# Sliding-window decode attention on one core: K and V in 32 KB rows, word transposes on VectorE, PV on four row groups

## The chip, the core and the metric

The kernel runs on one core of a Trainium2 chip. The core has a matrix engine (TensorE, "PE" in the profile, with its weight loads shown as "PEld"), VectorE ("DVE"), ScalarE ("ACT"), GpSimd ("POOL") and SyncE ("SP"), which here only issues transfers. 16 DMA engines carry data between HBM and the core's SBUF. Matmuls write PSUM, eight banks of 2 KB in each of 128 partitions; VectorE and ScalarE copy results out of it. The metric is the device time of one execution in microseconds; lower is better.

## What is computed

32 sequences each decode one token. The window is the last 512 keys of a cache of 2048. Four query heads share one key/value head (32 query heads, 8 KV heads, head size 128).

```python
W = min(4096, max(256, Sk // 4))                       # 512
q = (x @ wq).reshape(B, 1, 32, 128).transpose(0, 2, 1, 3)
k = jnp.repeat(k_cache[:, :, Sk - W:, :], 4, axis=1)
v = jnp.repeat(v_cache[:, :, Sk - W:, :], 4, axis=1)
p = softmax(einsum("bhqd,bhkd->bhqk", q, k) * 128 ** -0.5)
o = einsum("bhqk,bhkd->bhqd", p, v)
return o.transpose(0, 2, 1, 3).reshape(B, 1, 4096) @ wo
```

All arrays are bf16. The windows of K and of V are 33.5 MB each, wq and wo 4.2 MB each: 75.5 MB are read once.

## The kernel before

**Loads.** SP issues everything but x. The four pieces of wq (1 MB, rows of 8 KB) come first. Then `load_k(b)` (L136) and `load_v(b - 5)` (L144) alternate over the 32 batches, each in two halves of four KV heads, 512 KB in 128 rows of 4 KB: a partition holds 16 successive keys of one head (head c, key group s, with partition = 4 s + c). There are six K buffers and eight V buffers; a load waits until PE has finished with the batch that held its buffer. wo follows in eight pieces of 512 KB (L155), into the space of wq.

**Queries.** PE turns x, multiplies by wq with the weight columns as the stationary operand (L221), so that q comes out with the head dimension on the partitions; VectorE and ACT copy it to `QT_sb` (L353, L427). POOL lays each batch's q into `QBD` (L203), a zeroed block layout, so that eight matmuls give the scores of all heads of a batch.

**Scores.** For each batch, `transposes(b)` (L243) turns K in 32 PE transposes with a permutation as the moving operand, into four PSUM banks; VectorE copies three of these (L361) and ACT one (L435) into `KT_sb`. `scores(b)` (L260) multiplies 128 x 32 slices of `QBD` with 512 columns of `KT_sb`, four heads on four column groups of the array, and collects four batches in one bank `S_ps` of 128 rows (32 heads x 4 batches) by 512 keys.

**Softmax, for four batches ("a quad").** VectorE takes the row maximum (L367) and scales it (L369); ACT computes exp with the row sums (L443); VectorE takes the reciprocal (L375) and writes the normalised probabilities, spread out over four column slots, into `P_ex` (L383: four instructions of 32 partitions). PE transposes `P_ex` (L275), ACT copies it to `PT_sb` (L453).

**PV and output.** For each batch, 32 matmuls (L293) with V as the stationary operand (128 x 128) and 16 columns of `PT_sb`. VectorE copies the result, 32 columns, to `oT_sb` (L397). At the end band matmuls (L305) reorder `oT_sb` for the output projection (L337), 128 matmuls against wo; VectorE and ACT copy the result (L418, L473) and SP stores it (L161).

The engines run their own instruction lists in order; semaphores tie them together. On PE the order is transposes(it), scores(it - 1), pv_matmuls(it - 6), and every fourth iteration the transposes of P.

Of the kernel before, what the change touches and what calls it, by code (L numbers as in the profile page):

```python
# [12 lines left out]
def bass_standalone__sliding_block_cached__sampling_kernel(  # L13
# [15 lines left out]
    G = HKV  # L29
    G4 = 4  # L30
    NR = 16
    NS = 32
    DKT = D // 128
    SCALE = float(DH) ** -0.5
    P = 128

    NK = 6
    NV = 8
    NKT = 3
    NQB = 8  # L40
    LEAD = 5
    PVLAG = 6
    NQUAD = B // 4
    NHG = HQ // 4
    SELCUT = 28

    with ExitStack() as es:  # L47
        sb = lambda name, shape, dt: es.enter_context(nc.sbuf_tensor(name, shape, dt))
        ps = lambda name, shape, dt: es.enter_context(nc.psum_tensor(name, shape, dt))
        sem = lambda name: es.enter_context(nc.semaphore(name))  # L50

        w_sb = sb("w_sb", [P, DKT * HD], BF16)
        wq_sb = w_sb[:, :].rearrange("p (kt n) -> p kt n", kt=DKT)
        wo_sb = w_sb[:, :].rearrange("p (g i n) -> p g i n", g=NHG, i=4)
        K_sb = sb("K_sb", [P, NK, 2, NR, DH], BF16)
        V_sb = sb("V_sb", [P, NV, 2, NR, DH], BF16)
        KT_sb = sb("KT_sb", [P, NKT, 2, NR, G4, NS], BF16)
        QT_sb = sb("QT_sb", [P, HQ, B], BF16)
        QBD = sb("QBD", [P, NQB, G, 32], BF16)
        P_f32 = sb("P_f32", [P, W], F32)  # L60
        P_ex = sb("P_ex", [P, NR, NS, G4], BF16)
        PT_sb = sb("PT_sb", [P, 2, NR, P], BF16)
        oT_sb = sb("oT_sb", [P, HQ, B], BF16)
        o_sel = sb("o_sel", [P, 4, NHG, B], BF16)
        band = sb("band", [P, 4, 224], BF16)
        xT_sb = sb("xT_sb", [P, DKT, 32], BF16)
        ident = sb("ident", [P, P], BF16)
        perm = sb("perm", [P, G4, NS], BF16)
        x_sb = sb("x_sb", [32, D], BF16)
        out_sb = sb("out_sb", [32, 4, 128], BF16)  # L70
        maxv = sb("maxv", [P, NQUAD], F32)
        negmax = sb("negmax", [P, NQUAD], F32)
        sums = sb("sums", [P, NQUAD], F32)
        recip = sb("recip", [P, NQUAD], F32)
        junk = sb("junk", [P, 2], F32)

        KT_ps = ps("KT_ps", [P, 4, 1024], BF16)
        S_ps = ps("S_ps", [P, 512], F32)
        PT_ps = ps("PT_ps", [P, 2, 1024], BF16)
        QO_ps = ps("QO_ps", [P, 512], F32)  # L80
# [3 lines left out]
        sem_wo = [sem(f"sem_wo{i}") for i in range(NHG)]  # L84
        sem_k = [[sem(f"sem_k{i}_{h}") for h in range(2)] for i in range(NK)]
        sem_v = [sem(f"sem_v{i}") for i in range(NV)]
        sem_out = sem("sem_out")
        pe_xT = sem("pe_xT")
        pe_qt = sem("pe_qt")
        pe_T = [sem(f"pe_T{t}") for t in range(4)]  # L90
        pe_S = sem("pe_S")
        pe_PT = sem("pe_PT")
        pe_PV = sem("pe_PV")
        pe_fin = sem("pe_fin")
        pe_sel = sem("pe_sel")
        dve_sel = sem("dve_sel")
        act_sel = sem("act_sel")
        act_out = sem("act_out")
        pool_band = sem("pool_band")
        pool_perm = sem("pool_perm")  # L100
        pool_ex = sem("pool_ex")
        dve_xT = sem("dve_xT")
        dve_qt = sem("dve_qt")
        act_qt = sem("act_qt")
        dve_T = sem("dve_T")
        act_T = sem("act_T")
        dve_sm = sem("dve_sm")
        dve_sm2 = sem("dve_sm2")
        dve_P = sem("dve_P")
        dve_oT = sem("dve_oT")  # L110
        act_exp = sem("act_exp")
        act_PT = sem("act_PT")
        dve_out = sem("dve_out")
        act_warm = sem("act_warm")
        pool_init = sem("pool_init")
        pool_qbd = sem("pool_qbd")
        nc.scalar.dma_start(x_sb[:, :], x.rearrange("b s d -> b (s d)")).then_inc(sem_x, 16)
# [3 lines left out]
        def score_row(h, j):  # L121
            return 16 * h + 4 * j

        def cache_rows(cache, b, h):
            return cache[b, 4 * h:4 * h + 4, SK - W:, :].rearrange("g (s r) d -> s g (r d)", s=NS)

        @block.sync
        def _(sp):
# [3 lines left out]
            def load_k(b):  # L132
                if b >= NK:
                    sp.wait_ge(pe_T[3], b - NK + 1)
                for h in range(2):
                    sp.dma_start(  # L136
                        K_sb[:, b % NK, h].rearrange("p r d -> p (r d)"), cache_rows(k_cache, b, h)
                    ).then_inc(sem_k[b % NK][h], 16)

            def load_v(b):  # L140
                if b >= NV:
                    sp.wait_ge(pe_PV, b - NV + 1)
                for h in range(2):
                    sp.dma_start(  # L144
                        V_sb[:, b % NV, h].rearrange("p r d -> p (r d)"), cache_rows(v_cache, b, h)
                    ).then_inc(sem_v[b % NV], 16)

            for b in range(B + LEAD):
                if b < B:
                    load_k(b)  # L150
                if b >= LEAD:
                    load_v(b - LEAD)
            sp.wait_ge(pe_qt, 1)
            for hg in range(NHG):
                sp.dma_start(  # L155
                    wo_sb[:, hg].rearrange("p i n -> p (i n)"),
# [10 lines left out]
        def _(pool):  # L167
# [24 lines left out]
            for b in range(B):  # L192
                if b >= NQB:
                    pool.wait_ge(pe_S, b - NQB + 1)
# [309 lines left out]
```

## Time and profile before

| | |
|---|---|
| time of the runs | 195.83, 196.30, 196.42 us, median 196.3 |
| profiled execution, span | 194.7 us |
| PE matmul busy | 144.0 us (74%), 2724 matmuls |
| PE weight loads busy | 114.9 us (59%) |
| VectorE busy | 102.1 us (52%), 190 instructions |
| ScalarE busy | 57.6 us (30%), 70 instructions |
| GpSimd busy | 15.0 us (8%), 45 instructions |
| transfers | 75.97 MB in 20282 packets, mean 390 GB/s; the SP queue's take 97.2% of 16 engines' span |
| mean granted PE clock | 0.892 |

The span is the time from the first to the last instruction of one execution; the runs' times also contain what lies around it. A group line gives the source line, the engine, the operation, its output and inputs with shapes, the count, the busy time and the mean duration of one in ns, and after the bar the idle time of the engine just before these instructions with what ended it. A timeline line gives start and duration in us; neighbours of one group are merged with their count. A window line gives start and end of a stretch, then the busy time and number of instructions of PE, PEld, DVE, ACT and POOL, then the granted PE clock as a share of full speed, the DMA share and GB/s.

### The profile page before, as it was taken

The numbers are of one execution on the slowest core, as the hardware profiler recorded it, in microseconds if no ns is written. First come the engines' busy times: TensorE is split into PE (matmuls) and PEld (weight loads), VectorE is DVE, ScalarE is ACT, GpSimd is POOL, SyncE is SP. The second block draws the span as 40 slices with busy tenths as digits, with TensorE's granted clock in tenths as the row PEclk, the third lists the DMA queues.
The fourth block names the chain that finished last, engine by engine and source line by source line (L and its number), as shares of the span: only waits on it lengthen the run. The fifth ranks groups of instructions, "written<-read, shape, count | busy, mean of one in ns | idle before, by whom it ended". The sixth has DMA issues, their size and how long they took to land.

```text
span 194.7 us, 6153 instructions
## 1 busy us (share of the span) xinstructions
PE 144.0 (74%) x2724; PEld 114.9 (59%) x2724; DVE 102.1 (52%) x190; ACT 57.6 (30%) x70; POOL 15.0 (8%) x45
## 2 busy tenths in 40 slices
PE   0448995877897679749777988779776978937881
PEld 0337773755586567537555667557666667636760
DVE  0005778745684459533944587447943574670211
ACT  3001535622262126213252236204420352213101
POOL 8502000000020001000000000000000000000000
PEclk9999999999699978996999699979998887975558
DMA  5999999999999999999999999999999999999960
GB/s 204 426 420 406 412 405 411 407 410 407 409 407 407 408 408 410 407 407 410 407 407 410 409 407 407 410 406 408 408 406 411 405 410 405 412 405 412 406 251 31
DMA packets 20282, 75.97 MB, mean 390 GB/s; under 512 B 2272, under 2 KB 2336, under 8 KB 19744
## 3 DMA queue, kind: packets, MB, share of 16 engines
q1 hardware_dynamic: 20208, 75.54, 97.2%
q8 instruction: 22, 0.36, 0.8%
q10 hardware_dynamic: 48, 0.03, 0.1%
q14 instruction: 4, 0.03, 0.0%
HBM read 75.53 MB, written 0.03 MB: 388 GB/s over the span
## 4 chain that ended last, share of the span: by engine, by line
SPq 68%; DMA 23%; PE 5%; issue 3%; DVEq 0%; DVE 0%
SPq L144 37%; SPq L136 26%; DMA K_sb<-in_k_cache_dram 15%; DMA w_sb<-in_wo_dram 8%; SPq L155 5%; PE KT_ps L243 4%; SPq L130 1%; PE S_ps L260 1%; PE QO_ps L293 0%; PE KT_ps L337 0%; SPq L118 0%; DVEq L47 0%; DVE out_sb L418 0%
## 5 line engine op out<-in xcount | busy, mean ns | idle before, releaser
L243 PE MATMUL KT_ps<-perm,K_sb 128*128 128x128 bf16 x1024 | 75.2, 235 | 22.4 <-DMA K_sb<-in_k_cache_dram 22.2
L361 DVE COPY KT_sb<-KT_ps 128x1024 bf16<-128x1024 bf16 x96 | 63.6, 689 | 52.2 <-PE KT_ps L243 52.0
L243 PEld LDWEIGHTS KT_ps<-perm,K_sb 128*128 128x128 bf16 x1024 | 65.6, 106 | 30.0 <-DMA K_sb<-in_k_cache_dram 28.4
L435 ACT ACTIVATE KT_sb<-KT_ps 128x1024 bf16<-128x1024 bf16 x32 | 32.8, 1023 | 82.3 <-PE KT_ps L243 82.3
L293 PEld LDWEIGHTS QO_ps<-PT_sb,V_sb 128*128 128x128 bf16 x1024 | 28.3, 97 | 17.8 <-issue 13.5
L293 PE MATMUL QO_ps<-PT_sb,V_sb 128*128 128x16 bf16 x1024 | 31.1, 171 | 3.3 <-DMA V_sb<-in_v_cache_dram 1.3
L383 DVE TENSOR_SCALAR P_ex<-P_f,recip 32x512 bf16<-32x512 f32 x32 | 25.4, 793 | 1.2
L260 PE MATMUL S_ps<-KT_sb,QBD 128*32 128x512 bf16 x256 | 22.2, 428 | 0.0
L453 ACT ACTIVATE PT_sb<-PT_ps 128x1024 bf16<-128x1024 bf16 x16 | 15.5, 1021 | 19.4 <-PE PT_ps L275 19.4
L203 POOL COPY QBD<-QT_sb 128x32 bf16<-128x32 bf16 x32 | 8.5, 279 | 116.1 <-PE S_ps L260 108.1
L275 PE MATMUL PT_ps<-ident,P_ex 128*128 128x128 bf16 x128 | 9.4, 231 | 9.8 <-DVE P_ex L383 9.8
L275 PEld LDWEIGHTS PT_ps<-ident,P_ex 128*128 128x128 bf16 x128 | 7.9, 104 | 10.9 <-DVE P_ex L383 10.8
L397 DVE CAST oT_sb<-QO_ps 128x32 bf16<-128x32 f32 x32 | 9.3, 289 | 7.5 <-PE QO_ps L293 7.5
L221 PE MATMUL PT_ps<-xT_sb,w_sb 128*128 128x32 bf16 x128 | 4.1, 188 | 6.4 <-DMA w_sb<-in_wq_dram 6.4
L367 DVE TENSOR_REDUCE maxv<-S_ps 128x1 f32<-128x512 f32 x8 | 5.5, 691 | 5.4 <-PE S_ps L260 5.4
L221 PEld LDWEIGHTS PT_ps<-xT_sb,w_sb 128*128 128x128 bf16 x128 | 3.7, 104 | 6.8 <-DMA w_sb<-in_wq_dram 4.6
L443 ACT ACTIVATE P_f<-S_ps,negmax 128x512 f32<-128x512 f32 x8 | 5.5, 687 | 6.3 <-DVE negmax L369 6.3
L260 PEld LDWEIGHTS S_ps<-KT_sb,QBD 128*32 128x32 bf16 x256 | 3.9, 96 | 3.9 <-issue 1.4
L353 DVE CAST QT_sb<-PT_ps 128x512 bf16<-128x512 f32 x1 | 0.7, 691 | 10.3 <-PE PT_ps L221 10.3
L337 PE MATMUL KT_ps<-w_sb,o_sel 128*32 128x128 bf16 x128 | 3.8, 289 | 1.9 <-DMA w_sb<-in_wo_dram 1.5
L337 PEld LDWEIGHTS KT_ps<-w_sb,o_sel 128*32 128x32 bf16 x128 | 2.9, 131 | 2.7 <-DMA w_sb<-in_wo_dram 2.2
L427 ACT ACTIVATE QT_sb<-PT_ps 128x512 bf16<-128x512 f32 x1 | 0.6, 597 | 12.0 <-PE PT_ps L221 12.0
(28 smaller groups left out, 22.4 us busy)
## 6 DMA issues: line engine op xcount, KB each, us to landing
K_sb<-in_k_cache_dram SPq DMA_DIRECT2D x64, 512.0 KB, 15.6
V_sb<-in_v_cache_dram SPq DMA_DIRECT2D x64, 512.0 KB, 15.4
w_sb<-in_wq_dram SPq DMA_DIRECT2D x4, 1024.0 KB, 8.3
w_sb<-in_wo_dram SPq DMA_DIRECT2D x8, 512.0 KB, 15.4
x_sb<-in_x_dram ACTq DMA_DIRECT2D x1, 32.0 KB, 2.9
out_dram<-out_sb SPq DMA_DIRECT2D x1, 32.0 KB, 1.5
```

Source lines behind the costliest of these rows:

```text
L136: sp.dma_start(K_sb[:, b % NK, h].rearrange("p r d -> p (r d)"), cache_rows(k_cache, b, h)).then_inc(sem_k[b % NK][h], 16)
L144: sp.dma_start(V_sb[:, b % NV, h].rearrange("p r d -> p (r d)"), cache_rows(v_cache, b, h)).then_inc(sem_v[b % NV], 16)
L155: sp.dma_start(wo_sb[:, hg].rearrange("p i n -> p (i n)"), wo[hg * 512:(hg + 1) * 512, :].rearrange("(m i) n -> m (i n)", i=4),).then_inc( ...
L243: ins = pe.matmul(KT_ps[:, t, i * 128:(i + 1) * 128], lhsT=K_sb[:, b % NK, h, 8 * (t % 2) + i, :], rhs=perm[:, :, :], start=True, stop=Tru ...
L260: ins = pe.matmul(S_ps[32 * c:32 * c + 32, :], lhsT=QBD[:, b % NQB, g, :], rhs=KT_sb[:, b % NKT, h, :, c, :], start=(j == 0 and h == 0), s ...
L275: ins = pe.matmul(PT_ps[:, r // 8, (r % 8) * 128:(r % 8 + 1) * 128], lhsT=P_ex[:, r, :, :].rearrange("p s g -> p (s g)"), rhs=ident[:, :], ...
L293: ins = pe.matmul(QO_ps[:, 16 * h:16 * h + 16], lhsT=V_sb[:, b % NV, h, r, :], rhs=PT_sb[:, q % 2, r, :].rearrange("p (c n) -> p c n", c=G ...
L361: dve.tensor_copy(KT_sb[:, b % NKT, t // 2, 8 * (t % 2):8 * (t % 2) + 8, :, :], KT_ps[:, t, :]).then_inc(dve_T, 1)
L383: dve.tensor_scalar(P_ex[rows, :, :, c], P_f32[rows, :].rearrange("p (r s) -> p r s", r=NR), recip[rows, q:q + 1], None, op0=ALU.mult,).th ...
L397: dve.tensor_copy(oT_sb[:, :, b], QO_ps[:, 0:HQ]).then_inc(dve_oT, 1)
L435: act.activation(KT_sb[:, b % NKT, 1, 8:16, :, :], KT_ps[:, 3, :], ACTF.Copy).then_inc(act_T, 1)
L453: act.activation(PT_sb[:, q % 2, 8 * i:8 * i + 8, :].rearrange("p r n -> p (r n)"), PT_ps[:, i, :], ACTF.Copy,).then_inc(act_PT, 1)
```

## The change

The kernel is written anew around another layout. One step now handles a quad, four batches, and there are eight steps.

**Loads.** Partition 32 b + 4 h + k of a K or V buffer holds 128 successive keys of batch b of the quad, KV head h, key block k: one row of 32 KB. A load of K or V is one DMA of 4 MB; the last V comes in two halves. There are two buffers each for K and V. wq lies in the second V buffer, wo in the first K buffer, in four pieces of 16, 8, 4 and 4 rows of 1 KB for each partition. The order on SP is wq, K0, K1, V0, K2, V1, ..., K7, V6, V7, wo.

**Queries.** x, replicated four times over the columns, is now the stationary operand and wq streams with 512 columns (32 matmuls into all eight PSUM banks). The result lies with batches on the partitions; VectorE and ACT copy it to `Q_row`, and one VectorE transpose of 32 x 32 blocks of four-byte words (a word is two neighbouring bf16 of the head dimension) makes `QT_sb`. POOL fills `QBD` in four copies for each quad.

**Scores.** VectorE turns K by two such transposes for each quad, each of 4096 words in each partition; the writes step 512 B. Scores contract over 32 word positions of four batches at once, with even and odd halves apart, in 32 matmuls of 512 columns on four column groups.

**Softmax and PV.** The normalised P is written once in bf16; 16 matmuls with selection matrices (`spread_rows`) bring each score row to the partition layout of V; ACT compacts the result; eight VectorE multiplies with a head mask make `bd`, which is zero outside the own head. PV has `bd` (32 x 128) as the stationary operand and 512 columns of V streaming, on four row groups of 32 partitions, one for each batch, into four banks, 32 groups of keys. VectorE and ACT pick the diagonal blocks out (`pick`, two instructions each), and four fp32 matmuls (`fold`) sum over the key blocks and move heads to their places, so that ACT can write `o_sel` for the output projection directly.

```diff
+        K_sb = [sb(f"K_sb{i}", [P, R * DH], BF16) for i in range(2)]
+        V_sb = [sb(f"V_sb{i}", [P, R * DH], BF16) for i in range(2)]
+        KT_sb = sb("KT_sb", [P, 2, HKV, KB, R, 2], BF16)
...
+        def rows(cache, q, r0=0, r1=R):
+            return cache[4 * q:4 * q + 4, :, SK - W:, :].rearrange(
+                "b h (k r) d -> (b h) k (r d)", k=KB)[:, :, r0 * DH:r1 * DH]
...
+            def load_k(q):
+                if q >= 2:
+                    sp.wait_ge(s["dve_T"], 2 * (q - 2) + 2)
+                sp.dma_start(K_sb[q % 2][:, :], rows(k_cache, q)).then_inc(sem_k[q % 2], 16)
+            def load_v(q):
+                if q == 1:
+                    sp.wait_ge(s["pe_q"], 8)
+                if q >= 2:
+                    sp.wait_ge(s["pe_PV"], q - 1)
...
+            def turn(q):
+                dve.wait_ge(sem_k[q % 2], 16 * (q // 2 + 1))
+                if q >= 1:
+                    dve.wait_ge(s["pe_S"], q)
+                for w in range(2):
+                    dve.transpose(
+                        KT_sb[:, w].bitcast(F32).rearrange("p h k r t -> p r (h k t)"),
+                        K_sb[q % 2][:, :].bitcast(F32).rearrange(
+                            "p (r w c) -> p r w c", r=R, w=2)[:, :, w],
+                    ).then_inc(s["dve_T"], 1)
...
+            def scores(q):
...
+                for w in range(2):
+                    pe.wait_ge(s["dve_T"], 2 * q + w + 1)
+                    for t in range(2):
+                        for hh in range(2):
+                            for c in range(4):
+                                h = 2 * c + hh
+                                c0 = 32 * h - 16 * hh
+                                ins = pe.matmul(
+                                    S_ps[32 * c:32 * c + 32, :],
+                                    lhsT=QBD[:, q % 2, 2 * w + t, c0:c0 + 32],
+                                    rhs=KT_sb[:, w, h, :, :, t].rearrange("p k r -> p (k r)"),
...
+            def spread_rows(q):
+                pe.wait_ge(s["dve_P"], q + 1)
...
+                for e in range(REP):
+                    for k in range(KB):
+                        ins = pe.matmul(
+                            EP_ps[:, e * R:(e + 1) * R],
+                            lhsT=E_sb[:, k, e].rearrange("p m j -> p (m j)"),
+                            rhs=P_bf[:, k * R:(k + 1) * R],
...
+            def pv(q, g0, g1):
+                if g0 == 0:
+                    pe.wait_ge(s["dve_bd"], 8 * q + 8)
...
+                for g in range(g0, g1):
...
+                    for b in range(4):
+                        pr = slice(32 * b, 32 * b + 32)
+                        ins = pe.matmul(
+                            O_ps[:, b, :],
+                            lhsT=bd[pr, q % 2, 4 * g:4 * g + 4].rearrange("p r h e -> p (r h e)"),
+                            rhs=V_sb[q % 2][pr, 512 * g:512 * g + 512],
+                            start=g == 0, stop=g == R // 4 - 1, tile_position=(32 * b, 0),
+                        )
...
+            def fold(q):
...
+                pe.wait_ge(s["dve_C"], 2 * q + 2)
+                pe.wait_ge(s["act_C"], 2 * q + 2)
+                for d in range(4):
                     ins = pe.matmul(
+                        F_ps[:, 0:P],
+                        lhsT=F_sb[:, d].rearrange("p h d -> p (h d)"),
+                        rhs=C_sb[:, :, 32 * d:32 * d + 32],
...
+            for q in range(NQ + 1):
+                if q < NQ:
+                    scores(q)
+                if q >= 1:
+                    pv(q - 1, 0, 16)
+                if q < NQ:
+                    spread_rows(q)
+                if q >= 1:
+                    pv(q - 1, 16, 32)
+                    fold(q - 1)
...
+            def spread(q):
+                dve.wait_ge(s["act_pt"], q + 1)
...
+                for h in range(HKV):
                     dve.tensor_scalar(
+                        bd[:, q % 2, :, h, :], PTc[:, :, :], mask[:, h:h + 1], None, op0=ALU.mult
+                    ).then_inc(s["dve_bd"], 1)
+            def pick(q):
+                dve.wait_ge(s["pe_PV"], q + 1)
...
+                for r in range(2):
+                    pr = slice(32 * r, 32 * r + 32)
+                    dve.tensor_copy(
+                        C_sb[pr, :, :], O_ps[pr, :, r * DH:(r + 1) * DH]
+                    ).then_inc(s["dve_C"], 1)
+            for q in range(NQ):
+                turn(q)
+                maxes(q)
+                norm(q)
+                spread(q)
+                if q >= 1:
+                    pick(q - 1)
+            pick(NQ - 1)
```

`maxes`, `norm` and `do_exp` are the softmax of before on the quad's `S_ps`. ACT's order is exp(q), the compaction of q, its half of pick(q - 1), and the copy of fold(q - 1) to `o_sel`.

## The prediction

> **What bounds the kernel now.** I read the slices of the page first, then the chain that ended last, then the groups, then time windows.
>
> ```profile
> PEclk9999999999699978996999699979998887975558
> DMA  5999999999999999999999999999999999999960
> GB/s 204 426 420 406 412 405 411 407 410 407 409 407 407 408 408 410 407 407 410 407 407 410 409 407 407 410 406 408 408 406 411 405 410 405 412 405 412 406 251 31
> ...
> SPq 68%; DMA 23%; PE 5%; issue 3%; DVEq 0%; DVE 0%
> ```
>
> The transfers never pause: 408 GB/s from slice 4 on, and the chain is 91% DMA queue and transfers. PE (74%) and VectorE (52%) sit beside it. The first slices, when wq comes in 8 KB rows, run faster. The pieces of wq are consumed 2.49 us apart, and the end hangs on the last piece of wo:
>
> ```profile
> 11.09 1.03 PE L221 MATMUL PT_ps<-xT_sb,w_sb 128*128 128x32 bf16 x32 [1.46 <-DMA w_sb<-in_wq_dram]
> 13.57 1.04 PE L221 MATMUL PT_ps<-xT_sb,w_sb 128*128 128x32 bf16 x32 [1.45 <-DMA w_sb<-in_wq_dram]
> ...
> 191.66 0.41 PE L337 MATMUL KT_ps<-w_sb,o_sel 128*32 128x128 bf16 x16 [0.83 <-DMA w_sb<-in_wo_dram]
> 192.12 0.59 DVE L418 CAST out_sb<-KT_ps 32x128 bf16<-32x128 f32 x2 [5.39 <-PE KT_ps L337]
> 192.77 0.36 SPq L161 DMA_DIRECT2D out_dram<-out_sb  x1
> ```
>
> 1.049 MB in 2.49 us is 421 GB/s. After the last wo piece (191.66) 3.04 us remain. The profiled span is 194.7; the median of the runs is 196.3, so 1.6 us lie outside the span and are added to every sum.
>
> **What the change gives the transfers.** At 408 GB/s each of 16 engines takes 0.1606 us for a 4 KB packet, at 421 GB/s 0.3113 us for 8 KB: 0.1507 per 4 KB and 0.010 per packet. A 32 KB row would take 8 x 0.1507 + 0.010 = 1.216 us, 431 GB/s (bounds: 408, no gain; 440, no packet cost). A 4.19 MB load takes 9.72 us. wq ends at 13.55 as now, K and V (67.1 MB) at 169.2, wo (16, 8, 4 and 4 KB rows) 9.9 later at 179.1; with 3.04 the span is 182.1, the time 184. That is 12 us of gain if all else hides. The PE transposes (75.2 us), their copies (63.6 on VectorE, 32.8 on ACT) and the PV loads go too, but they were hidden.
>
> **What it puts on a chain.** VectorE's order for four batches q is turn(q), max, normalise, eight masked copies, pick(q-1), then turn(q+1). PE's is scores(q), half of PV(q-1), spread_rows(q), the other half, fold. pick(q-1) waits for the second half of PV, which waits in PE's queue behind spread_rows(q) and scores(q), which need turn(q). So turn, PE's stream and pick run one after the other, once per quad. One more turn cannot start early: it is behind pick in VectorE's queue. Call this period C; transfers need 2 x 9.72 = 19.45.
>
> ```profile
> L361 DVE COPY KT_sb<-KT_ps 128x1024 bf16<-128x1024 bf16 x96 | 63.6, 689 | 52.2 <-PE KT_ps L243 52.0
> L383 DVE TENSOR_SCALAR P_ex<-P_f,recip 32x512 bf16<-32x512 f32 x32 | 25.4, 793 | 1.2
> L367 DVE TENSOR_REDUCE maxv<-S_ps 128x1 f32<-128x512 f32 x8 | 5.5, 691 | 5.4 <-PE S_ps L260 5.4
> ...
> 56.84 0.29 DVE L397 CAST oT_sb<-QO_ps 128x32 bf16<-128x32 f32 x1
> 56.94 1.30 DVE L361 COPY KT_sb<-KT_ps 128x1024 bf16<-128x1024 bf16 x2
> ...
> 21.07 0.61 PE L260 MATMUL S_ps<-KT_sb,QBD 128*32 128x512 bf16 x8
> ...
> 89.56 1.04 PE L260 MATMUL S_ps<-KT_sb,QBD 128*32 128x512 bf16 x8
> ```
>
> *Turn.* Two transposes of 4096 four-byte words per partition. No row shows a transpose. Four-byte reads at L367 (512 in 691 ns) and the 128-element cast at L349 (292 ns) give 1.04 ns a word and 0.158 us fixed. The bf16 copy of L361 does two elements in that time (0.5 ns each), the fast bound. The slow bound is L397, 32 elements written 64 B apart: 289 ns, or (289 - 158)/32 = 4.1 ns each. But the next copy starts 0.10 us after L397 and is no longer than usual (two copies in 1.30), so I read the excess as latency, and take 1.04, the four-byte row: 4.26 + 0.075 (start to start) and 4.26 + 0.158, in all 8.76, with 0.05 to PE 8.81. [...]
>
> *PE.* Eight 512-column matmuls on four column groups take 0.61 us: two rounds of 0.213 and 0.18 of drain, so four groups do run together. Scores of the second half, 16, are 4 rounds, 0.85. PV is 128 matmuls with four row groups: no row shows row groups. Together they are 32 rounds, 6.83; one after another 27.3 (third rival). I take the first, as L260 is the nearest row. [...] Spread_rows is 16 matmuls like L243's (16 in 1.07): 0.91. With drain 8.77. The softmax between (max 0.73, scale 0.18, exp and sum 0.83, reciprocal 0.25, normalise 0.55, hand-overs) is 2.6 and lies under the 3.41 of PV's first half.
>
> *Masked copies.* Compaction on ACT 0.65 (L427's 597 ns and hand-over), then eight 512-element multiplies, bf16 to bf16: between 0.21 (four per cycle) and 0.82 (L383 start to start); I take L361's two per cycle, 0.34, so 2.8. Together 3.5, hidden by PV's second half (3.4 + 0.18); at 0.82 they would add 3.8 us a quad. *Pick*: two of 0.69 (512 f32 from PSUM), with hand-overs 1.5.
>
> C with PE at full clock: 8.81 + 8.77 + 1.5 = 19.1, already about the transfers' 19.45.
>
> *Clock.* It won't stay full:
>
> ```profile
> 88.00:89.00 1.00, 1.00 (x13) 1.00 (x11) 0.19 (x1) 0.00 (x0) 0.00 (x0) 0.50 1.02 406
> 90.00:91.00 1.00, 1.00 (x25) 0.47 (x18) 0.35 (x1) 0.75 (x1) 0.23 (x1) 0.50 1.04 414
> 91.00:92.00 1.00, 1.00 (x32) 1.00 (x29) 0.49 (x2) 0.44 (x1) 0.00 (x0) 0.95 1.02 406
> ...
> 174.59 1.89 PE L275 MATMUL PT_ps<-ident,P_ex 128*128 128x128 bf16 x16 [2.18 <-DVE P_ex L383]
> ```
>
> (The last three columns are granted clock, DMA share, GB/s.) From 84.0 to 87.6 PE was busy 1.07 us of 3.4, and from 87.6 to 91.1 it was granted 0.50 though busy. L260 then takes 1.04 for 0.61. A burst of 1.89 us at 174.59 did not lift it. In the new order PE has only the fold and 16 first-half scores in the 10.3 us of pick and turn, so it falls each time. If it comes back after one full 3.4 us stretch of work, that is 3.4 to 6.8 us after the second scores begin, on average 5.1, half lost: 2.5 us. **C = 21.6** (19.1 to 27.7, all slow).
>
> **Sum.** K(0) lands at 13.55 + 9.72 = 23.3. Q is ready by then: wq's last 8 matmuls end at 15.5, four copies each on VectorE and ACT at 16.5, Q's transpose (2048 words, 2.3) at 18.8, POOL's four copies (128 elements, (279 - 99)/32 = 5.6 ns each from L203 and L180, 0.8 each) at 22.1; later they lie under C, and the constants before them under wq. turn(0) to 32.1, slow scores 1.9, softmax 2.6, slow spread_rows 1.9, compaction and copies 3.5: turn(1) starts at 42.0, 9 us behind K(1) (33.0). Six times 21.6: turn(7) at 171.6. Then 8.8 + 11.3 + 1.5 (to 193.2), fold(6) 1.0 (four fp32 matmuls that no row shows; 0.2 as bf16, 1.8 with four slow passes), PV(7) whole 7.0, pick 1.5, fold 1.0, copy 0.4 (204.1), output projection 4.0 (96 of L337 take 3.00 between 186.78 and 189.78), copies 0.7, store 1.93 as now: 210.7, and 1.6 outside: **212.3**. wo, queued behind V(7), has landed by about 192, so its cut into pieces is worth nothing here. Buffers cost nothing: K(q+2) waits for turn(q) and has C to land; V likewise.
>
> The forecast's own range is 195 (clock up, 7 x 2.5 less) to 238 (slow masked copies, or the clock down through most of PV).
>
> **Rivals.**
> 1. *Faster: the word transposes run at two words a cycle*, as L361's copies. A turn is 4.5, C 17.3, below 19.45, and the lag is made up. Then K(7) lands at 33.0 + 6 x 19.45 = 149.7 and the last chain, 39.1 - 4.3 = 34.8, ends at 184.5: 186. It beats the kernel of before once eight turns save 16.6 us, a turn under 6.7. For it: L361. Against: those are 2-byte elements. 20%.
> 2. *Scattered writes are slow.* Between 1.04 and L397's 4.1 ns a word lie all prices; at the middle by ratio, 2.1, eight turns are 8.7 us longer each: 282; at 4.1, 25: over 400. For it L397's length, against it its start to start. 15%.
> 3. *The row groups don't run together*, so the change doesn't do what it says: 8 x 20.5 more, 376; a third of that already leaves the range. Nothing in the page shows row groups; L260 speaks against it. 4%.
>
> **How the numbers follow.** The forecast has 61%, of it 2% within the first 0.3% or just under. Its time is 212.3. The range goes down to rival 1's 184 (transfers alone) and up to 240; it leaves out rivals 2 and 3, 19%. 0.3% is about what a measurement here can tell from no change. Faster 0.21 (rival 1 and the best of the forecast), same 0.02, slower 0.77.
>
> **What would show it.** Right: two transposes of about 4.4 us a quad, a chain of waits that is VectorE and PE rather than DMA queue, DMA slices well below 9 in the middle, 19 to 24 us between turns, packets of 32 KB at about 431 GB/s while they run, clock near 0.5 at the start of PV. Wrong: transposes near 2.2 us, DMA still full and the end hung on wo (rival 1), transposes of 8 us or more (rival 2), a PV half of 13 us (rival 3).

## The result and the profile after

The changed kernel takes **256.0 us** (median of four runs, 255.57 to 256.71) against 196.3 before: a ratio of 1.304 (95% interval 1.301 to 1.307), slower by 30%. The prediction was 212.3 with a range of 184 to 240; the time lies 16 us above the range. The direction was right, the size was not. In three of the later kernels some executions ran slower at a lower granted clock: the medians and ranges below count them, the ratios leave them out.

The slices of the page after, and the share of the chain of waits by engine:

```profile
PEclk9996555555895569655975589557955597559999
DMA  6999999998899289856987397919993008993000
GB/s 262 482 418 413 423 459 428 423 413 317 356 348 449 103 336 381 361 250 248 413 333 330 103 453 274 459 57 390 338 413 165 1 3 343 441 410 130 3 3 8
...
DVE 52%; PE 41%; issue 2%; DMA 2%; ACT 1%; ACTq 0%; DVEq 0%
```

Before, DMA stood at 9 in all but the first and the last two slices and the chain was 91% DMA queue and transfers. Now DMA has holes from slice 10 on, down to 1 and 3 GB/s, the mean is 299 GB/s, and the chain is VectorE and PE with 2% of DMA. The transfers wait for the engines. SP, which issues them, waits 116.0 us for K buffers that VectorE has not yet turned and 81.3 for V buffers that PE has not finished. The longest of its rows (us in total, times, longest):

```profile
SPq L115 <- DVE KT_sb L353: 116.0, 6, 33.0
```

So far that is what the prediction said would show it right. The groups say by how much it was wrong (mean ns of one after the comma):

```profile
L353 DVE STREAM_TRANSPOSE KT_sb<-K_sb 128x4096 f32<-128x4096 f32 x16 | 113.1, 7143 | 0.2
L267 PE MATMUL ps<-V_sb,bd 32*128 32x512 bf16 x1024 | 68.0, 422 | 0.0
L384 DVE TENSOR_SCALAR bd<-PTc,mask 128x512 bf16<-128x512 bf16 x64 | 17.6, 350 | 37.8 <-ACT PTc L435 37.8
L435 ACT ACTIVATE PTc<-ps 128x512 bf16<-128x512 f32 x8 | 10.5, 1310 | 32.7 <-PE ps L244 32.7
```

One transpose takes 7.14 us where the prediction took 4.3 to 4.4: (7143 - 158)/4096 = 1.70 ns a word instead of 1.04. One whole period in the chain of waits (start, duration, what):

```profile
155.76 14.18 DVE KT_sb L353 x2
169.98 1.90 PE ps L226 x16
171.88 5.12 PE ps L267 x55
177.00 1.00 PE ps L244 x16
178.00 3.59 PE ps L267 x64
181.65 0.67 issue
182.33 0.68 DVE C_sb L394
183.04 14.16 DVE KT_sb L353 x2
```

The order is the predicted one: turn, scores, half of PV, spread_rows, the other half, pick, and only then the next turn. The period is 183.04 - 155.76 = 27.28 us; without the turn it is 13.1, where the prediction had 21.6 - 8.81 = 12.8. The turn's two transposes take 14.14 instead of 8.76, 5.38 more; eight of them are 43.0 us, and the span, 253.9, lies 43.2 above the predicted 210.7. Nearly all of the miss is one price.

The clock was lost as predicted. Two stretches of one period (columns as in the profile before; the last three are granted clock, DMA share, GB/s):

```profile
115.50:117.40 1.90, 1.85 (x20) 0.47 (x24) 0.00 (x0) 0.00 (x0) 0.00 (x0) 0.50 0.92 241
120.30:122.40 2.10, 2.10 (x40) 0.82 (x32) 0.00 (x0) 0.00 (x0) 0.00 (x0) 0.98 0.76 328
```

The scores after the turn run at 0.50, and the clock is back some 5 us later, at 120.3, so the first half of PV takes 5.1 us and the second 3.6.

### The profile page after: what moved, and what is told of

Same layout as the page of the kernel before. It is cut to its first block, busy times and chain, and to the rows that moved or that the text cites. A ratio compares the mean times of both kernels' runs of the same rounds, so it can differ in the third digit from the quotient of the medians.

```text
span 253.9 us, 3687 instructions
## 1 busy us (share of the span) xinstructions
PE 127.4 (50%) x1636; PEld 56.5 (22%) x1636; DVE 161.9 (64%) x143; ACT 36.1 (14%) x56; POOL 16.9 (7%) x52
## 2 busy tenths in 40 slices
DMA packets 3729, 75.80 MB, mean 299 GB/s; under 512 B 449, under 2 KB 513, under 8 KB 769
## 4 chain that ended last, share of the span: by engine, by line
DVE 52%; PE 41%; issue 2%; DMA 2%; ACT 1%; ACTq 0%; DVEq 0%
DVE KT_sb L353 45%; PE ps L267 26%; PE ps L226 6%; PE ps L244 4%; PE ps L205 3%; DVE C_sb L394 3%; DMA x_sb<-in_x_dram 2%; DVE QT_sb L342 1%; DVE KT_sb L339 1%; PE ps L284 1%; PE ps L307 1%; DVE bd L384 1%; ACT PTc L435 1%; ACTq L97 0%; ACT P_f L426 0%
## 5 line engine op out<-in xcount | busy, mean ns | idle before, releaser
L353 DVE STREAM_TRANSPOSE KT_sb<-K_sb 128x4096 f32<-128x4096 f32 x16 | 113.1, 7143 | 0.2
L226 PE MATMUL ps<-KT_sb,QBD 128*32 128x512 bf16 x256 | 30.4, 623 | 99.3 <-DVE KT_sb L353 99.3
L267 PE MATMUL ps<-V_sb,bd 32*128 32x512 bf16 x1024 | 68.0, 422 | 0.0
L384 DVE TENSOR_SCALAR bd<-PTc,mask 128x512 bf16<-128x512 bf16 x64 | 17.6, 350 | 37.8 <-ACT PTc L435 37.8
L267 PEld LDWEIGHTS ps<-V_sb,bd 32*128 32x128 bf16 x1024 | 27.3, 103 | 40.1 <-issue 19.0
L394 DVE COPY C_sb<-ps 32x512 f32<-32x512 f32 x16 | 10.9, 681 | 8.8 <-PE ps L267 8.3
L435 ACT ACTIVATE PTc<-ps 128x512 bf16<-128x512 f32 x8 | 10.5, 1310 | 32.7 <-PE ps L244 32.7
L446 ACT ACTIVATE C_sb<-ps 32x512 f32<-32x512 f32 x16 | 9.4, 588 | 22.4 <-PE ps L267 22.2
L244 PE MATMUL ps<-P_bf,E_sb 128*128 128x128 bf16 x128 | 9.4, 231 | 2.5 <-DVE P_bf L373 2.5
L205 PE MATMUL ps<-V_sb,xT_sb 128*128 128x512 bf16 x32 | 9.6, 475 | 0.8 <-DVE xT_sb L318 0.8
```

What stands on the lines that cost most here:

```text
L205: ins = pe.matmul(ps[:, n], lhsT=xT_sb[:, kt, :], rhs=wq_sb[:, kt, n * 512:(n + 1) * 512], start=kt == 0, stop=kt == DKT - 1, tile_positio ...
L226: ins = pe.matmul(S_ps[32 * c:32 * c + 32, :], lhsT=QBD[:, q % 2, 2 * w + t, c0:c0 + 32], rhs=KT_sb[:, w, h, :, :, t].rearrange("p k r -> ...
L244: ins = pe.matmul(EP_ps[:, e * R:(e + 1) * R], lhsT=E_sb[:, k, e].rearrange("p m j -> p (m j)"), rhs=P_bf[:, k * R:(k + 1) * R], start=k = ...
L267: ins = pe.matmul(O_ps[:, b, :], lhsT=bd[pr, q % 2, 4 * g:4 * g + 4].rearrange("p r h e -> p (r h e)"), rhs=V_sb[q % 2][pr, 512 * g:512 * ...
L353: dve.transpose(KT_sb[:, w].bitcast(F32).rearrange("p h k r t -> p r (h k t)"), K_sb[q % 2][:, :].bitcast(F32).rearrange("p (r w c) -> p r ...
L384: dve.tensor_scalar(bd[:, q % 2, :, h, :], PTc[:, :, :], mask[:, h:h + 1], None, op0=ALU.mult).then_inc(s["dve_bd"], 1)
```

## The experiments

What is open is why a word transpose takes 7.1 us, and whether the rest of the sum is right for the right reason. My theory after the result (theory A below): the writes step 512 B, and that costs 2.7 us for 4096 words. In two of the expectations a line is a stretch of 16 B that every word of a wide step would open anew: a supposition of mine, of which the runs show only the times at each step. Rivals: a word transpose takes 1.7 ns a word however it is written; the source, read in runs of 32 words with gaps, is what slows it; the half clock of PE, not the turn, is most of the loss.

### The write made contiguous

`KT_sb` is laid out so that each block of 32 words is written in one run; the scores then read it in runs of four elements, and `spread_rows` takes P with a step of 8 B.

```diff
-        KT_sb = sb("KT_sb", [P, 2, HKV, KB, R, 2], BF16)
+        KT_sb = sb("KT_sb", [P, 2, R, HKV, KB, 2], BF16)
-                                    rhs=KT_sb[:, w, h, :, :, t].rearrange("p k r -> p (k r)"),
+                                    rhs=KT_sb[:, w, :, h, :, t],
-                            rhs=P_bf[:, k * R:(k + 1) * R],
+                            rhs=P_bf[:, :].rearrange("p (r k) -> p k r", k=KB)[:, k, :],
-                        KT_sb[:, w].bitcast(F32).rearrange("p h k r t -> p r (h k t)"),
+                        KT_sb[:, w].bitcast(F32).rearrange("p r h k t -> p r (h k t)"),
```

> The K transposes write their 32 words next to each other (the buffer's key dimension outermost), and the scores read them back as runs of four bf16 4 B apart in steps of 128 B; columns then stand in the order (key, block), and spread_rows picks its block with a step. Theory A (scattered writes cost the 0.66 ns a word over 1.04): a transpose takes 4.4 us instead of 7.14, a quad's period 27.2 - 5.4 = 21.8, the time about 256 - 8 x 5.4 = 213, if the scores' matmuls keep 1.9 us for 16. Theory B (the transpose itself takes 1.7 ns a word whatever it writes to): transposes stay 7.1, time 256. Theory C (the scores pay for the strided read instead): transposes 4.4, but 16 score matmuls take longer than 1.9, up to 4 us, time 213 to 230.

Measured: 219.88 us (219.46 to 220.01), ratio to before 1.119 (1.117 to 1.121). Two groups of its page:

```profile
L353 DVE STREAM_TRANSPOSE KT_sb<-K_sb 128x4096 f32<-128x4096 f32 x16 | 70.2, 4423 | 0.2
L244 PE MATMUL ps<-P_bf,E_sb 128*128 128x128 bf16 x128 | 16.1, 294 | 2.5 <-DVE P_bf L373 2.5
```

The transpose falls to 4.42 us, the price that the prediction took; the rival of a fixed 1.7 ns a word is out. The scores' 16 matmuls stay at 1.90 us, their time at a clock of 0.50 in the changed kernel, so at the half clock reading in runs of four costs them nothing. Nor does it at full clock: in the last kernel below, which has this layout, 16 of them take 1.05 us, and contiguous columns take 1.08 in the kernel that keeps the clock up.

```profile
164.47 1.05 PE L233 MATMUL ps<-KT_sb,QBD 128*32 128x512 bf16 x16
```

But the time is some 7 us above what the transposes alone would give: the `spread_rows` matmuls went from a mean of 231 to 294 ns, 16 of them from 1.07 to 2.02 us at a granted clock of 1.00 (window columns as before):

```profile
102.20:104.10 1.90, 1.90 (x20) 1.71 (x16) 0.00 (x0) 0.00 (x0) 0.00 (x0) 1.00 1.04 448
```

In the first quad, where the clock of the changed kernel is 0.50, the step costs little: 2.03 us for 1.90. That is tried by itself below.

### How wide a step the write bears

In these two kernels only the write's step changes, in one transpose of each pair to one value and in the other to the other (st is the step in words).

```diff
+                    st = (4, 16)[w]
                     dve.transpose(
-                        KT_sb[:, w].bitcast(F32).rearrange("p h k r t -> p r (h k t)"),
+                        KT_sb[:, w].bitcast(F32).rearrange("p h k r t -> p (h k r t)").rearrange(
+                            "p (a x b) -> p a b x", x=32, b=st),
                         K_sb[q % 2][:, :].bitcast(F32).rearrange(
-                            "p (r w c) -> p r w c", r=R, w=2)[:, :, w],
+                            "p (a b w c) -> p a b w c", b=st, w=2, c=32)[:, :, :, w],
```

> The transposes write with other steps: the first of each turn 16 B between words, the second 64 B; the words land elsewhere, so the scores and the output are not the reference's. Theory A in the form that each word opens a new line: both 7.1. Theory A in the form that large steps cost more: 16 B cheaper than 64 B, and 64 B below or at 7.1. Theory B: both 7.1, so it is told from A by the contiguous write, not here.

> As the run with steps of 16 and 64 B, with 8 B (two words in 16 B) for the first transpose of each turn and 4 B (contiguous blocks) for the second; scores and output are not the reference's. If what costs is the change of a 16 B line at every word, 8 B takes 4.4 to 5.5 us and 4 B 4.4; if any step costs, 8 B takes 7.1. Time between 220 and 256 accordingly.

Measured: 258.75 us with steps of 16 and 64 B, 212.60 us with 8 and 4 B (one run each). The view of the transposes' line, duration in ns as min/median/max, first of the wider steps, then of the narrower:

```profile
L354 DVE STREAM_TRANSPOSE KT_sb<-K_sb x16: 7064/7324/7511, 23.4 to 219.4; 128x4096 f32<-128x4096 f32 x16
```
```profile
L354 DVE STREAM_TRANSPOSE KT_sb<-K_sb x16: 4401/4422/4447, 23.4 to 176.0; 128x4096 f32<-128x4096 f32 x16
```

There is a cliff, not a slope: 4 B and 8 B give 4.42 us, 16 B and 64 B give 7.1 to 7.5, as do the 512 B of the changed kernel. No step between 8 and 16 B was tried, so the edge itself is not located. The price beyond it is 2.7 us on 4.4, a factor of 1.6. This is measured for the four-byte writes of VectorE's transposes; PE's read of P in steps of 8 B, above, does pay (2.02 us for 1.07).

The second kernel is also the best test of the rest of the sum, since it differs from the changed kernel in that price alone. Three turns in its chain of waits:

```profile
23.44 8.78 DVE KT_sb L354 x2
...
42.13 8.69 DVE KT_sb L354 x2
...
171.60 8.78 DVE KT_sb L354 x2
```

Predicted were 23.3, 42.0 and, for the last, 171.6. Single periods lie between 20.9 and 22.4, their mean is 21.58 (21.6 predicted). The span is 210.7, as predicted, and the time 212.6 against 212.3.

### Transposes and copies, and the source

One transpose of each pair becomes a plain copy with the same scattered write; the other keeps its write and reads a contiguous source.

```diff
+                    if w == 0:
+                        dve.tensor_copy(
                             KT_sb[:, w].bitcast(F32).rearrange("p h k r t -> p r (h k t)"),
...
+                    else:
+                        dve.transpose(
...
+                            K_sb[q % 2][:, :].bitcast(F32)[:, 0:R * 32].rearrange(
+                                "p (r c) -> p r c", r=R),
```

> In each turn the first transpose is a plain copy of words with the same source and the same scattered destination, the second a transpose that reads a contiguous half of the K buffer and writes scattered as before; the scores, and so the output, are not the reference's. Theory A (scattered writes): the copy takes about 7.1 us too, the second transpose stays 7.1. Theory B (the transpose itself): the copy takes 4.4 (one word a cycle) or 2.3 (two), the second transpose 7.1. Theory D (the source's 128 B runs cost): the second transpose drops to 4.4 and the copy stays near 7.1.

In a second kernel both are copies, the first written contiguously, the second with a 16 B step.

```diff
+                    if w == 0:
+                        dve.tensor_copy(
+                            KT_sb[:, w].bitcast(F32).rearrange("p h k r t -> p (h k r t)").rearrange(
+                                "p (r c) -> p r c", r=R),
...
+                    else:
+                        dve.tensor_copy(
+                            KT_sb[:, w].bitcast(F32).rearrange("p h k r t -> p (h k r t)").rearrange(
+                                "p (a x b) -> p a b x", x=32, b=4),
```

> Leaves out: K is not turned, both transposes are replaced by copies of the same 4096 four-byte words, the first written contiguously, the second with a 16 B step; so the scores are not the reference's. If a scattered write costs a copy as much extra as it costs the transpose (2.7 us for 4096), the contiguous copy takes about 4.75 - 2.7 = 2.05 us, two words a cycle, and the 16 B step about 4.7. If a four-byte copy goes at one word a cycle however it is written, both take 4.4 to 4.75 and the scatter penalty belongs to the transpose alone. Time by the first 212.3 - 8 x 2.0 = about 196 us or more, bounded by transfers from then on; by the second about 213 to 216.

Measured: 234.16 us and 192.80 us (one run each). The groups of the first kernel, then of the second:

```profile
L360 DVE STREAM_TRANSPOSE KT_sb<-K_sb 128x4096 f32<-128x4096 f32 x8 | 57.8, 7223 | 0.0
...
L354 DVE COPY KT_sb<-K_sb 128x4096 f32<-128x4096 f32 x8 | 38.0, 4749 | 0.2
```
```profile
L361 DVE COPY KT_sb<-K_sb 128x4096 f32<-128x4096 f32 x8 | 31.0, 3878 | 0.0
...
L354 DVE COPY KT_sb<-K_sb 128x4096 f32<-128x4096 f32 x8 | 18.3, 2293 | 0.2
```

The contiguous source changes nothing (7.22 us): the rival of the read is out. A copy of the same words takes 2.29 us when written contiguously, 0.56 ns a word, so a four-byte copy does have the price of the first rival; 3.88 with a 16 B step and 4.75 with 512 B. So a plain copy pays for scattering too, 1.6 and 2.5 us, and only part of this was expected: my theory had put the 512 B copy at 7.1, as long as the transpose, and the 16 B step at 4.4 or more. For a copy the price grows from 16 to 512 B; the transposes showed 7.06 to 7.51 over all wide steps. Why the two operations differ there stays open.

The second kernel also tries the first rival's threshold with a turn of 2.29 + 3.88 = 6.2 us. The prediction said that such a kernel beats the one before once a turn is under 6.7; 192.8 against 196.2 agrees (about 196 was expected here). It was the transpose that could not have that price.

### P read in steps, or written in the order in which it is read

The contiguous kernel again, but the normalise instruction writes P by key blocks, so that `spread_rows` reads contiguous columns.

```diff
-                            rhs=P_bf[:, :].rearrange("p (r k) -> p k r", k=KB)[:, k, :],
+                            rhs=P_bf[:, k * R:(k + 1) * R],
-                    P_bf[:, :], P_f32[:, :], recip[:, q:q + 1], None, op0=ALU.mult
+                    P_bf[:, :].rearrange("p (k r) -> p k r", k=KB),
+                    P_f32[:, :].rearrange("p (r k) -> p k r", k=KB), recip[:, q:q + 1], None, op0=ALU.mult
```

> The contiguous write as in the earlier kernel, and the normalise instruction writes P in the order of the key blocks, so that spread_rows reads contiguous columns. If the stepped read of P_bf is what kept the earlier kernel at 219.9: sixteen spread_rows matmuls fall from 2.02 to about 1.07 us at full clock and the group's mean from 294 to about 219-231 ns, the normalise grows from 486 to 680 ns, so each of eight quads is 0.95 - 0.19 = 0.76 us shorter: 219.9 - 6.1 = 213.8 us (212 to 215). If the longer spread_rows had another cause: they stay at 2.0 us and the time is 221 us.

Measured: 211.70 us (211.40 to 212.01), ratio 1.079 (1.076 to 1.081).

```profile
L244 PE MATMUL ps<-P_bf,E_sb 128*128 128x128 bf16 x128 | 9.4, 231 | 2.7 <-DVE P_bf L373 2.7
...
L373 DVE TENSOR_SCALAR P_bf<-P_f,recip 128x512 bf16<-128x512 f32 x8 | 5.4, 677 | 0.3
```

The matmuls are back at 231 ns, so the stepped moving operand was what doubled them. The time fell by 8.2 us, not 6.1, and lies just below the 212 that I had given as the lowest. I had charged the longer normalise (677 for 486 ns) to the path, but from the second quad on it ends while PE is still in the first half of PV: at 0.95 us in each of these seven quads the gain is 6.7. Most of the rest is PV's first halves, 1.3 us shorter in all in this profile; their length hangs on when the clock comes back (4.0 to 5.7 us in these two kernels). A contiguous turn without any other gain is thus still 8% slower than before.

### The clock kept up

The scattered transposes stay; PE multiplies into a bank that nothing else uses yet, while it waits for them, 24 matmuls ahead of the first half of the scores and 22 ahead of the second.

```diff
+            def keep(n):
+                for _ in range(n):
+                    pe.matmul(
+                        Y_ps[:, :],
...
+                    if q >= 1:
+                        keep(24 if w == 0 else 22)
```

> PE gets idle work (24 and 22 matmuls of 512 columns into the unused output bank) while it waits for the first and second transpose of each turn from the second quad on. My reading of the clock (a quad loses 0.9 us in the second scores and 1.5 in PV's first half because PE was idle before): 16 scores take 1.0 instead of 1.9, PV's first half 3.6 instead of 5.1, a period 24.8 to 25.0 instead of 27.2, time 256 - 7 x 2.4 = 239. Rival (the clock falls for another reason, or the idle work itself delays the scores): no change or slower.

Measured: 242.38 us (241.93 to 242.63), ratio 1.234 (1.233 to 1.236). PE's timeline:

```profile
112.62 1.08 PE L237 MATMUL ps<-KT_sb,QBD 128*32 128x512 bf16 x16 [1.17 <-DVE KT_sb L364]
113.63 3.63 PE L278 MATMUL ps<-V_sb,bd 32*128 32x512 bf16 x64
```

The scores fall from 1.90 to 1.08 us and the first half of PV from 5.1 to 3.63; a period is 25.1 us instead of 27.3. 239 was expected; the transposes take 7.24 us here instead of 7.14, 1.5 us in all, for a reason that stays open. The lost clock costs about 13.6 us in all, 2.2 a period where the prediction took 2.5. It is a real term, but not the one that was missing: the rival of the clock leaves 242.

### The order of VectorE

Still scattered. VectorE does the first transpose of the next quad right after normalising, and PE the first half of PV before the second half of the scores.

```diff
-                turn(q)
                 maxes(q)
                 norm(q)
+                if q + 1 < NQ:
+                    turn(q + 1, 0)
                 spread(q)
                 if q >= 1:
                     pick(q - 1)
+                if q + 1 < NQ:
+                    turn(q + 1, 1)
```

> The scattered transposes stay; only the order changes: VectorE does the next quad's first transpose right after normalising, while PE runs PV, and PE does PV's first half before the second scores. My chain theory (turn, PE stream and pick one after the other set the period; a transpose beside PV leaves the chain): the period is 7.1 (second transpose) + 1.5 (scores) + 2.6 (softmax) + 7.1 (first transpose, over PV) + 2.2 (masked copies) + 1.4 (pick) = 22.0 instead of 27.2, time 256 - 7 x 5.2 = 220. Rival (the transposes slow down beside PE or beside transfers, or VectorE's total of 20 us a quad with its waits binds): 230 to 256.

Measured: 216.02 us (214.92 to 218.26), ratio 1.097 (1.094 to 1.100). VectorE's transposes in its timeline:

```profile
93.40 7.29 DVE L359 STREAM_TRANSPOSE KT_sb<-K_sb 128x4096 f32<-128x4096 f32 x1
...
104.21 7.21 DVE L359 STREAM_TRANSPOSE KT_sb<-K_sb 128x4096 f32<-128x4096 f32 x1
...
114.72 7.30 DVE L359 STREAM_TRANSPOSE KT_sb<-K_sb 128x4096 f32<-128x4096 f32 x1
```

The first and the last line are the second transposes of two successive quads, the middle one is a first. They cost what they did, but the period is 21.3 us (114.72 - 93.40; 22.0 and a time of 220 were expected). The order alone is worth 40 us: half of the turn then lies beside PE's work. This shows the step of the prediction that pick, behind PV's second half and ahead of the next turn in VectorE's queue, puts everything in a row.

### Towards a kernel that beats both

The order, the contiguous write, P by key blocks, PV in parts of 12, 12 and 8 rounds, and x loaded in one transfer instead of four:

```diff
-        for i in range(4):
-            nc.scalar.dma_start(
-                x_sb[8 * i:8 * i + 8, :], x[8 * i:8 * i + 8].rearrange("b s d -> b (s d)")
-            ).then_inc(sem_x, 16)
+        nc.scalar.dma_start(x_sb[:, :], x.rearrange("b s d -> b (s d)")).then_inc(sem_x, 16)
...
+                    pv(q - 1, 0, 12)
...
+                    scores(q, 1)
...
+                    pv(q - 1, 12, 24)
```

> The same order with transposes that write contiguously; the normalised P is written block by block so that spread_rows reads it contiguously; x comes in one transfer. Chain theory: the period 4.4 + 1.5 + 2.6 + 4.4 + 2.2 + 1.4 = 16.5 falls below the 19.45 that the transfers need at 431 GB/s, so DMA is full again to the end and the time is K(7)'s landing at 150 plus about 38 to 40 of last chain and 1.6: 189 to 192, below the 196.2 of before. Rival 1 (transfers in 32 KB rows give no more than the 408 GB/s of 4 KB rows): about 198. Rival 2 (another wait holds the chain, period above 19.45): over 196.

Measured: 196.25 us (194.35 to 198.22, 12 runs), ratio 0.996 (0.994 to 0.999).

```profile
DMA  5999999999999999999999999999999999997000
GB/s 212 428 445 431 431 431 431 431 431 428 431 428 431 431 428 426 431 431 428 428 431 431 428 433 431 435 425 435 425 431 428 438 416 425 425 413 322 13 0 10
...
DMA 52%; DVE 23%; PE 14%; issue 8%; ACT 1%; SPq 1%; DVEq 0%
...
L356 DVE STREAM_TRANSPOSE KT_sb<-K_sb 128x4096 f32<-128x4096 f32 x16 | 71.0, 4442 | 12.2 <-DMA K_sb<-in_k_cache_dram 12.0
```

Now the transfers never pause (428 to 431 GB/s in most slices) and VectorE waits 12.0 us for K instead of the reverse. But the last K lands at 152.1 and 42.3 us follow, where I had expected 38 to 40 after an earlier landing.

The next kernel takes the fold out of the end of a step, so that fold(6) no longer stands ahead of all of the last PV; the third adds idle matmuls around the last fold:

```diff
+                    if q >= 2:
+                        fold(q - 2)
...
-                    fold(q - 1)
+            keep(7)
+            fold(NQ - 1)
+            keep(4)
```

> As order_contig, but PE does the fold of a quad one step later, behind the next first scores, and the last fold but one in the middle of the last PV, so that PE no longer waits for pick before the first scores. With DMA full until wo has landed, only the chain after K(7) counts (42.3 us in order_contig): the last second scores start 2.4 us earlier (when the transpose is done, not 2.5 after) and a fold of 1.1 leaves it: 196.2 - 3.4 = 192.8. Rival (the end hangs on something else, or PV is only pushed back): 196, no change.

> As fold_later, with 7 and 4 idle matmuls into the score bank after the last PV and after the last fold. The output projection took 3.46 us at the half clock in order_contig and 1.97 in the changed kernel: 1.4 us less than fold_later, 191.4. Rival (the clock falls all the same, or the idle matmuls delay the fold): the same as fold_later or a little slower.

Measured: 196.87 us (196.63 to 197.33), ratio 1.003 (1.002 to 1.005), without `keep`; 195.26 (193.06 to 196.42), ratio 0.988 (0.985 to 0.991), with it. Both missed what was expected, the first by 4 us, the second by 2.6 (0.988 x 196.4 = 194.0, and 191.4 was expected): in the profiles of both, the first 48 matmuls of the last PV took 5.31 us, in the first at a granted clock of 0.50. The last kernel puts 12 idle matmuls after each step's PV and 7 ahead of each fold as well.

```diff
                     if q >= 2:
+                        keep(7)
                         fold(q - 2)
...
                     pv(q - 1, 24, 32)
+                    if q < NQ:
+                        keep(12)
```

> As fold_later_end_kept, with idle matmuls into the output bank in every step too: 12 after each PV and 7 before each fold, so that PE does not fall to the half clock. In fold_later the last PV ran its first 48 matmuls in 5.3 us instead of 2.7 and PV's first part before the last second scores 4.0 instead of 2.7; this clock, not the fold, would be why the later fold gained nothing. Theory: the last second scores start 1.3 us earlier, the last PV is 2.7 us shorter, the projection stays 2.0: 194.8 - 4.0 and 1.6 outside, 192.4, with all runs together instead of spread over 193 to 196. Rival: the idle work pushes the scores back by as much, 195 to 197.

Measured: **192.84 us** (192.43 to 193.81), ratio 0.985 (0.983 to 0.987). The first 48 matmuls of the last PV, in the timeline without idle matmuls and in the one with them everywhere:

```profile
175.65 5.31 PE L266 MATMUL ps<-V_sb,bd 32*128 32x512 bf16 x48 [3.14 <-DVE C_sb L402]
```
```profile
174.28 2.77 PE L275 MATMUL ps<-V_sb,bd 32*128 32x512 bf16 x48 [0.44 <-issue]
```

In the first of the two the granted clock is 1.00 before the 3.14 us of waiting for the pick and 0.50 after:

```profile
170.60:172.50 1.90, 1.90 (x34) 0.74 (x32) 0.44 (x2) 1.31 (x1) 0.00 (x0) 1.00 0.97 414
...
175.70:178.50 2.80, 2.80 (x28) 1.18 (x32) 0.00 (x0) 0.00 (x0) 0.00 (x0) 0.50 0.90 364
```

The 48 matmuls then take 5.31 us; with the gap filled they take 2.77. The length of the wait alone doesn't decide it: the kernel with the fold at the end has the same 3.14 us, and there the clock is 1.00 after it too.

```profile
176.74 1.13 PE L283 MATMUL ps<-C_sb,F_sb 128*128 128x128 f32 x8 [3.14 <-DVE C_sb L398]
177.80 7.08 PE L266 MATMUL ps<-V_sb,bd 32*128 32x512 bf16 x128
```

What decides it is not shown; the idle matmuls remove the doubt. The last kernel beats both, the one before by 1.5%. In the profiled execution its span is 190.6 us, 8.5 above the 182.1 of the transfers alone.

## Why the prediction was wrong, and where it was right

**The step that failed** is the price of the word transpose in the turn: "take 1.04, the four-byte row". It is 1.70 ns for writes 512 B apart, and 1.04 (4.42 us for 4096) for writes 4 or 8 B apart. The trace of before had a row that warned of it, L397 at 289 ns for 32 scattered elements, and the prediction read its excess as latency because the next copy started 0.10 us later. That reading was an argument and no run had shown it. Nor does the row give the price: at 1.70 ns a word it would take 212 ns, and what the other 77 are stays open. The second rival, that scattered writes are slow, had the cause right, but was priced at 2.1 ns or more and kept out of the range; the point between, 1.7, was priced in no case. With ends of 1.04 and 4.1 ns for a cost that counts 16 times on the chain, the range should have held more of the second: 1.7 ns adds 43 us by the prediction's own formula.

**The chain** was right: turn, PE and pick in a row, no buffer that binds. Changing the order alone took 40 us off with the price unchanged.

**The other terms** were mostly right. With the transposes at 4.42 us the same program takes 212.6. That this is within 0.3 us of the forecast is partly luck, since some errors cancel (next paragraph). The four row groups run together: 64 matmuls of 512 columns take 3.63 us, 16 rounds of 0.213 and some drain (0.213 is worked out from L260's 0.61 and 1.04 us before, two rounds at full and at half clock), and the third rival falls. In the last, uncovered PV 128 matmuls take 7.05 us in the chain of waits, at a granted clock of 1.00; one after another they would be 27.3 by that round, an estimate, so they run 3.9 times as fast.

```profile
238.83 7.05 PE ps L267 x128
```

The half clock costs 2.2 us a period (2.5 predicted).

**Small terms off, without weight.** The masked copies start 0.27 us apart (2.19 for eight, 2.8 predicted) and ACT's compaction takes 1.31 (0.65): together 3.5, as predicted. The four matmul calls of a fold take 1.13 us at full clock (1.0). The prediction's lower bound for a masked copy (0.21) and its upper one for a fold (1.8) are shown by no run. The output projection is 1.97 us at a clock of 1.00, not 4.0; in the kernel with steps of 8 and 4 B it is 3.40, and the last slice of the page, in which most of it lies, has a clock of 0.7. o_sel's copy is 0.73, not 0.4. Q's transpose ends at 23.69 instead of 18.8: x landed late, so that the matmuls with wq end near 19.0 and not at 15.5, and the transpose takes 3.61 instead of 2.3; its writes step 256 B, and (3612 - 158)/2048 is 1.69 ns a word. But K(0) was due at 23.3, and turn(0) starts just 0.4 us late. Three figures of the prediction are off in themselves, also without weight: without packet cost its own numbers give 435 GB/s, not 440; from 84.0 to 87.6 are 3.6 us, not 3.4 (3.4 is the length of the stretch at 0.50 that follows, 87.7 to 91.1); and to beat the kernel before, eight turns must save 16.0 us, not 16.6.

**The gain that was expected of 32 KB rows** agrees with what is measured, 428 to 431 GB/s where the transfers run without a pause (431 predicted), but the changed kernel can't use it: transfers are hidden behind a chain of VectorE and PE, and 75.80 MB go at a mean of 299 GB/s.

## What to carry to other kernels

Let VectorE's transposes write their four-byte words 8 B apart or closer (4.42 us for 4096, against 7.06 to 7.51 at the steps of 16 B and more that were tried), and turn the stride over to the reader, if that one bears it: the scores' matmuls did (runs of four, 1.05 us for 16 at full clock), the matmul with a plain 8 B step did not (2.02 us for 1.07). Two-byte elements written 8 B apart were slow on ACT and on VectorE (next section). When work moves to an engine that was idle, write down its whole order in one period, and see whether the new work can start before the last result of the period is in: here that was worth 40 us, about as much as the price of the operation (43). Where two rows of the profile bound a price that counts on every step, the range has to hold both, whatever speaks for one.

## What the hardware showed that was not expected

- VectorE's transpose of 4096 four-byte words: 4.42 us for writes at 4 B, 8 B or in runs, 7.06 to 7.51 us at 16 B, 64 B and 512 B. A plain copy: 2.29 us contiguous, 3.88 at 16 B, 4.75 at 512 B.
- A bf16 moving operand in steps of 8 B nearly doubled 16 matmuls of 128 columns at full clock, 2.02 us for 1.07; in the first quad, where the clock of the changed kernel is 0.50, they took 2.03 for 1.90.
- ACT writing 512 elements 8 B apart took 1310 ns, and 597 contiguously in the trace of before; it pays at a step that VectorE's transposes of four-byte words bore. VectorE, too, took 793 ns for 512 bf16 written 8 B apart (L383 before) and 486 contiguously (L373 after).
- x in four transfers was there for PE at 8.0 us, in one at 3.8 before and at 4.4 in the kernel with the new order and contiguous writes. The stages behind it hid that.
- Taking work off the end of a chain can lengthen what is left: with the fold moved, the clock fell during a wait of 3.14 us and 48 matmuls took 5.31 us instead of 2.77. With the fold at the end the same wait left the clock at 1.00.
